# Keeping the MLP's residual in DRAM and adding it at the end, with 1/std spread over the partitions by a DMA instead of by TensorE

## The chip, the cores and the metric

One core of a Trainium2 chip runs one program: a decayed linear attention, an MLP behind a layer norm, and a small mixture of causal attention heads, all in float32 or in pairs of rounded float32 values. The metric is the device time of the program in microseconds.

## The reference, cut to what matters

```python
x = attn_out.transpose(0, 2, 1, 3).reshape(B, S, H * D)      # 2 x 768 x 512, output of the linear attention
mu  = np.mean(x, axis=-1, keepdims=True)
var = np.mean((x - mu) ** 2, axis=-1, keepdims=True)
xn  = (x - mu) / np.sqrt(var + 1e-06) * g_ln
x   = x + np.maximum(xn @ w_ch1, 0.0) @ w_ch2                # w_ch1: 512 x 2048, w_ch2: 2048 x 512
...                                                          # then gate, q, k, v, four attention heads, output product
```

Because ReLU commutes with a positive factor, `1/std` of a row can be put on the MLP's result instead of on its input: with `d = (x - mu) * g_ln`, the row's new `x` is `x + (relu(d @ w_ch1) @ w_ch2) / std`.

## The kernel before

Activations lie transposed in SBUF. The tile `xT` (`xpool`, line 309) holds all 1536 rows as 128 partitions x 4 slices of the model dimension x 1536 columns. The columns are four blocks of 384 (`TB`); `KS` (line 408) cuts the four slices into two halves, so that most VectorE and ScalarE work comes as 128 x 768 pieces (two slices of one block).

**Three stages.** First the linear attention (twelve steps `n`, one for each chunk of 128 rows), which ends with `ret_copy` (line 396): ScalarE copies from PSUM into `xT`. With it, as soon as a block of `xT` is whole, go the four norm steps `ln_a` to `ln_d` of that block, the preparation of weights (`prep_parts`, line 204) and the first MLP products. Second the MLP: `g1` (line 486) makes a group of the hidden layer, one `h` of 128 x 384 by 12 matmuls, and its `leave` turns it into the pair `hs` by ScalarE's ReLU and a VectorE subtraction; `g2` (line 519) multiplies four of these by the second weight, into a double PSUM bank `y` of 128 x 2 x 384, and its `leave` (line 532) adds `y` to `xT` on VectorE. The very first such sum, group 0 of block 0, is made piecemeal by `g2f` (line 539) in the two banks `yf0`, `yf1`. Third come the projections and the attention (`qkv_steps`, `att_s` and so on).

**The norm's factor.** `ln_d` (line 461) leaves `std` and `rs = 1/std` of a block as columns: 128 partitions x 3. `columns` (line 453) makes three matmuls with the identity out of such a column tile, which spread it as a row over all partitions in a PSUM tile (`sb` for std, `rb` for 1/std). Ahead of the block's first sum, `ln_e` (line 473) multiplies `xT` by std; the sums of all four groups are then added; `x2_split` (line 678) at the end multiplies by 1/std, and splits the result into the pair `x2` (ScalarE's cast, VectorE's subtraction, `split`, line 200). So residual and MLP sum live in one tile, at the price of one product ahead and one behind.

**What sets the order.** TensorE's order is that of the program text throughout. The other engines' order is the text's up to `by_hand.close()` (line 664) and a scheduler's after that. The weights come by SyncE's queue (`load_w`, line 122) into three buffers `raw` of pool `stage`; each is prepared in parts (`mag` on ScalarE, seven VectorE operations, the cast `w` on ScalarE), and the next load waits until VectorE has read the buffer. The PSUM tag `big` has two buffers, which `yf0`, `yf1` and then the `y` use in turn: a `y` can begin when the last but one has been taken out of PSUM.

Of the kernel before, what the change touches and what calls it, by code (L numbers as in the profile page):

```python
# [8 lines left out]
F32 = mybir.dt.float32  # L9
# [5 lines left out]
ALU = mybir.AluOpType  # L15
AX = mybir.AxisListType

P = 128
# [4 lines left out]
KT = DM // P  # L23
DFF = 2048
FT = DFF // P
TB = 384
NBLK = B * S // TB
NTB = TB // P
GF = 4
# [38 lines left out]
def model(ctx, tc, qkT, kv, lam, g_ln, w12, wat, out):  # L68
    nc = tc.nc
# [10 lines left out]
    stage = mp.enter_context(tc.tile_pool(name="stage", bufs=3))  # L80
    dec64 = mp.enter_context(tc.tile_pool(name="dec64", bufs=2))
    lnp = mp.enter_context(tc.tile_pool(name="lnp", bufs=2))
    psum = ctx.enter_context(tc.tile_pool(name="psum", bufs=1, space=bass.MemoryType.PSUM))
    dram = ctx.enter_context(tc.tile_pool(name="dram", bufs=1, space=bass.MemoryType.DRAM))
# [7 lines left out]
    def ps_mid(name):  # L92
        return psum.tile([P, 512], F32, tag="mid", bufs=4, name=name)
# [78 lines left out]
    n, free_at = PLAN_FROM, 0  # L172
    while rest:
        for p in rest:
            ft, i = p
# [5 lines left out]
        else:  # L181
            p = None
# [6 lines left out]
    pieces = first + [plan[n] for n in sorted(plan)]  # L189
    to_load = [lambda p=p: load_w(*p) for p in pieces] + [lambda i=i: load_wa(i) for i in range(4)]  # L190

    def load_next(k=1):
        for _ in range(k):
            if to_load:
                to_load.pop(0)()
# [4 lines left out]
    def split(dst_hi, dst_lo, src):  # L200
        nc.scalar.copy(dst_hi, src)
        nc.vector.tensor_tensor(dst_lo, src, dst_hi.bitcast(F32), ALU.subtract)
# [43 lines left out]
    second = []  # L246
# [157 lines left out]
            nc.scalar.copy(x[half(h2), 1], po[half(1 - h2), 1])  # L404


    XN, LN, DQ, SCALED = {}, {}, {}, set()
    KS = (ts(0, 2), ts(2, 4))

    def ln_parts(blk, src, name):  # L410
# [39 lines left out]
    def ln_c(blk):  # L450
        LN[blk] = ln_parts(blk, DQ[blk], "va")

    def columns(col, name):

        ps = ps_mid(name)
        for c in range(NTB):
            nc.tensor.matmul(ps[:, c * P:(c + 1) * P], col[:, c:c + 1].to_broadcast([P, P]), ident,
                             start=True, stop=True, skip_group_check=True)
        return ps[:, None, :TB].to_broadcast([P, 2, TB])

    def ln_d(blk):

        ps = ps_mid(f"var{blk}")
        for c in range(NTB):
            nc.tensor.matmul(ps[:, c:c + 1], LN[blk][:, c * P:(c + 1) * P], part_w[:, :1], start=True, stop=True,
                             skip_group_check=True)
        std = lnp.tile([P, NTB], F32, tag="std", name=f"std{blk}", bufs=NBLK)
        nc.scalar.activation(std, ps[:, :NTB], AF.Sqrt, bias=eps_sb)
        rs = lnp.tile([P, NTB], F32, tag="rs", name=f"rs{blk}", bufs=NBLK)
        nc.vector.reciprocal(rs, std)  # L470
        LN[blk] = (std, rs)

    def ln_e(blk):

        by = columns(LN[blk][0], f"sb{blk}")

        def times(ks):
            x = xT[:, ks, blk * TB:(blk + 1) * TB]
            nc.vector.tensor_tensor(x, x, by, ALU.mult)

        return [(1.0, lambda: times(KS[0])), (1.0, lambda: times(KS[1])), (0.0, lambda: SCALED.add(blk))]


    PASSES = ((0, 0), (1, 0), (0, 1))
    HS, LAST, HXT, HDQ = {}, [], [], []
# [33 lines left out]
    def g2(g, blk, half):  # L519

        y = ps_big(f"y{g}{blk}{half}")
        for f in range(GF):
            w = W[g * GF + f, 1]
            h = HS[g * GF + f, blk]
            for j in range(2):
                e = 2 * half + j
                for i, (wi, xi) in enumerate(PASSES):
                    nc.tensor.matmul(y[:, j, :TB], w[:, wi, e * P:(e + 1) * P], h[:, xi],  # L528
                                     start=(f == 0 and i == 0), stop=(f == GF - 1 and i == 2))
        xv = xT[:, 2 * half:2 * half + 2, blk * TB:(blk + 1) * TB]  # L530

        def leave():
            nc.vector.tensor_tensor(xv, xv, y[:, :, :TB], ALU.add)  # L533

        return leave

# [2 lines left out]
    def g2f(g, blk, f):  # L539

        if f == 0:
            YF.extend(ps_big(f"yf{j}") for j in range(2))
        w = W[g * GF + f, 1]
        h = HS[g * GF + f, blk]
        for e in range(KT):
            for i, (wi, xi) in enumerate(PASSES):
                nc.tensor.matmul(YF[e // 2][:, e % 2, :TB], w[:, wi, e * P:(e + 1) * P], h[:, xi],  # L547
                                 start=(f == 0 and i == 0), stop=(f == GF - 1 and i == 2))

        def leave():  # L550
            if f == GF - 1:
                for j in range(2):
                    xv = xT[:, 2 * j:2 * j + 2, blk * TB:(blk + 1) * TB]
                    nc.vector.tensor_tensor(xv, xv, YF[j][:, :, :TB], ALU.add)

        return leave

# [17 lines left out]
    def mlp_step():  # L575
        n = len(steps) - len(todo)
        due = [k for k in plan if k <= n]
        if due:
            plan.pop(min(due))
        decode(1 if due else 0)  # L580
        for blk in range(1, NBLK):
            if todo[0] == ("g2", 0, blk, 0):
                for _, scale in ln_e(blk):
                    scale()
        f, args, leave = step()
        leave()
        return f, args
# [4 lines left out]

    later_parts = []
    for ft in range(GF):
        if ft == GF - 1:
            later_parts.append((2.0, lambda: [f() for _, f in ln_e(0)]))
        later_parts += prep_parts(ft, 1)

    def room(us):
# [5 lines left out]
    def ready(k, inside):  # L605
        f, g, blk, j = todo[k]
        if f == "g1":
            return blk in XN and (g * GF + j, 0) in W and not (inside and (j, blk) in IN_WA)
        return f == "g2f" and (g * GF + j, 1) in W and (j < GF - 1 or blk in SCALED) and not inside

    def next_step(inside):

# [10 lines left out]
    while n < len(order) or min(norm_at) < 4 or norm_parts or weight_parts:  # L623
        if n < len(order):
            if n + 3 < len(order):
                ret_load(*order[n + 3])
                if n < 2:
                    load_next()
            if n + 1 < len(order):
                ret_scores(n + 1)  # L630
            ret_outer(n)
            ret_state(n)
            ret_inner(n)
            if n + 1 < len(order):
                ret_decay(n + 1)
            if n + 1 < len(order):
                ret_qd(n + 1)
            ret_sum(n)
            ret_copy(n)

        for blk in range(NBLK):
            if n >= NTB * (blk + 1) and norm_at[blk] < 4 and not (norm_at[blk] == 2 and blk not in XN) \
                    and not (norm_at[blk] == 1 and blk > 0 and norm_at[blk - 1] < 3):
                norm_parts += (ln_a, ln_b, ln_c, ln_d)[norm_at[blk]](blk) or []
                norm_at[blk] += 1
        if n < len(order):
            leave = next_step(True) if n >= MLP_FROM else None
            if n > 0:
                room(ROOM[leave is not None])
            if leave:  # L650
                leave()
        if n == len(order) - 1:
            rp.close()
            ap_ = ctx.enter_context(tc.tile_pool(name="ap", bufs=HX, side="right", reuse_waits="tile"))
            WPOOL2[0] = mp.enter_context(tc.tile_pool(name="wpool2", bufs=1, side="right", reuse_waits="tile"))
            weight_parts += later_parts
        if n >= len(order):
            for _ in range(2):
                leave = next_step(False)
                room(ROOM_MLP)  # L660
                if leave:
                    leave()
        n += 1
# [5 lines left out]
    def split_wa(i):  # L669
        raw, n = WRAW[i]  # L670
        w = ap_.tile([P, 2, 1040], F32R, tag="wa", name=f"wa{i}") if i < HX else             xnp.tile([P, 2, 1040], F32R, tag="dq", name=f"wa{i}", bufs=1)
        for c in (ts(0, 512), ts(512, n)):
            split(w[:, 0, c], w[:, 1, c], raw[:, c])
        WA.append(w[:, :, :n])
# [2 lines left out]

    def x2_split(blk):
        x2 = xnp.tile([P, 2, KT, TB], F32R, tag="xn", name=f"x2_{blk}")
        by = columns(LN.pop(blk)[1], f"rb{blk}")  # L680
        for ks in KS:
            x = xT[:, ks, blk * TB:(blk + 1) * TB]
            nc.vector.tensor_tensor(x, x, by, ALU.mult)
            split(x2[:, 0, ks], x2[:, 1, ks], xT[:, ks, blk * TB:(blk + 1) * TB])
        X2[blk] = x2

    wa_jobs = [lambda i=i: split_wa(i) for i in range(4)]
    while todo:
        f, args = mlp_step()
        if not pieces and not second and to_load:  # L690
            load_next()
        elif not pieces and not second and wa_jobs and len(todo) % 2 == 0:
            wa_jobs.pop(0)()
        if f == "g2" and args[0] == NG - 1 and args[2] == 1:
            x2_split(args[1])
    for job in wa_jobs:
        job()
# [274 lines left out]
```

## Time and profile before

| | us |
|---|---|
| median of 3 runs (474.23, 476.39, 476.47) | 476.39 |
| the profiled execution's own time | 477.41 |
| its span in the profile | 475.6 |
| TensorE busy (97% of the span) | 462.1 |
| VectorE busy (71%) | 340.0 |
| ScalarE busy (43%) | 202.9 |
| GpSimd busy (18%) | 86.0 |
| DMA: bytes read, written | 31.47 MB, 3.15 MB |

A row of the chain or of a timeline reads: start in us, duration in us, engine, line of the kernel, operation, output <- input, count, and in brackets the idle time of the engine ahead of it and what ended that. Several instructions may be merged into one row. Matmuls overlap in their records: one of the 128 x 128 identity products shows 274 ns, but they follow each other much closer, so the chain, not the busy time, tells what a matmul costs. SPq and ACTq are the queues' DMA instructions on SyncE and ScalarE. A float32 matmul appears as two records.

### The profile page before, as it was taken

How to read it: one execution, taken by the hardware profiler on the slowest of the kernel's cores; microseconds unless marked ns; L12 is line 12 of the kernel's file. 1: busy time of each engine (PE TensorE's matmuls, PEld its weight loads, DVE VectorE, ACT ScalarE, POOL GpSimd, SP SyncE). 2: the span in 40 equal slices, each digit the busy share in tenths (PEclk: the TensorE clock that was granted, in tenths of full speed). 3: DMA queues.
4: the chain of work that ended last, by engine and by line, in shares of the span. 5: the costliest groups of instructions: out<-in, count | busy, mean ns of one | idle time of the engine just before them, and what ended most of it. 6: DMA issues, size and time to landing. Idle time of an engine off the chain costs nothing.

```text
span 475.6 us, 9173 instructions
## 1 busy us (share of the span) xinstructions
PE 462.1 (97%) x3630; PEld 430.8 (91%) x3630; DVE 340.0 (71%) x707; ACT 202.9 (43%) x471; POOL 86.0 (18%) x132
## 2 busy tenths in 40 slices
PE   6799999999999999999999999999999999999996
PEld 4676779999999999999999999999998898998885
DVE  4688888979999787626789725435679686586663
ACT  2558675412334222202234312212356666647672
POOL 6556400000000000000000000000055444344340
PEclk8999999999999999999999999999999999999999
DMA  7986211222232231201233200000000000000011
GB/s 283 370 308 234 97 45 45 90 88 74 90 109 92 91 124 46 89 1 44 65 113 96 83 1 0 2 1 1 1 0 1 24 22 24 23 1 33 36 46 66
DMA packets 10842, 35.20 MB, mean 74 GB/s; under 512 B 1456, under 2 KB 1712, under 8 KB 10800
## 3 DMA queue, kind: packets, MB, share of 16 engines
q1 hardware_dynamic: 10512, 34.49, 21.1%
q8 instruction: 28, 0.46, 0.4%
q10 hardware_dynamic: 288, 0.13, 0.1%
q14 instruction: 14, 0.11, 0.1%
HBM read 31.47 MB, written 3.15 MB: 73 GB/s over the span
## 4 chain that ended last, share of the span: by engine, by line
PE 84%; DVE 9%; ACT 4%; DMA 1%; issue 1%; POOL 0%; SPq 0%; ACTq 0%; DVEq 0%
PE h L494 27%; PE y L528 26%; PE pj L730 4%; PE s L810 4%; PE av L859 4%; PE o L880 4%; PE t L847 4%; PE pv L752 3%; PE yf L547 2%; DVE a L347 2%; DMA qk<-in_qkT 1%; PE sc L326 1%; DVE xn L440 1%; PE po L378 1%; DVE qs L738 1%
## 5 line engine op out<-in xcount | busy, mean ns | idle before, releaser
L494 PE MATMUL h<-xn,w 128*128 128x384 f32 x768 | 140.0, 336 | 0.0
L494 PEld LDWEIGHTS h<-xn,w 128*128 128x128 f32 x768 | 133.3, 188 | 3.1 <-PE va L414 0.6
L528 PE MATMUL y<-hs,w 128*128 128x384 f32 x552 | 99.8, 334 | 0.0
L528 PEld LDWEIGHTS y<-hs,w 128*128 128x128 f32 x552 | 96.1, 188 | 0.0
L513 ACT ACTIVATE hs<-h 128x384 fp32r<-128x384 f32 x50 | 24.5, 490 | 103.0 <-PE h L494 89.4
L744 POOL TENSOR_SCALAR kh<-kh 64x384 fp32r<-64x384 f32 x16 | 8.4, 524 | 299.8 <-DVE qs L738 288.2
L514 DVE SCALAR_TENSOR_TENSOR hs<-h,hs 128x384 fp32r<-128x384 f32 x50 | 27.7, 555 | 41.4 <-ACT hs L513 41.4
L533 DVE TENSOR_TENSOR xT<-xT,y 128x768 f32<-128x768 f32 x30 | 28.5, 951 | 31.6 <-PE y L528 31.6
L837 POOL TENSOR_SCALAR att<-att,c,gw 128x128 f32<-128x128 f32 (+5 forms) x48 | 35.8, 750 | 51.7 <-DVE c L834 16.3
L229 ACT CAST w<-top 128x512 fp32r<-128x512 f32 x32 | 19.9, 620 | 52.9 <-DVE top L223 50.9
L730 PE MATMUL pj<-x,wa 128*128 128x384 f32 x192 | 35.0, 337 | 0.0
L730 PEld LDWEIGHTS pj<-x,wa 128*128 128x128 f32 x192 | 33.4, 188 | 0.0
L848 ACT COPY aT<-t 128x512 f32<-128x512 f32 (+3 forms) x64 | 26.5, 442 | 11.1 <-PE t L847 10.8
L847 PE MATMUL t<-ident,att 128*128 128x128 f32 x168 | 26.2, 275 | 0.5 <-DVE qs L738 0.5
L214 ACT ACTIVATE mag<-raw 128x512 f32<-128x512 f32 x32 | 21.1, 666 | 7.1 <-DVE w L241 7.1
L859 PE MATMUL av<-aT,v 128*64 128x128 f32 x336 | 23.6, 280 | 0.0
L810 PE MATMUL s<-kh,qs 128*128 128x512 f32 (+3 forms) x64 | 23.3, 366 | 0.0
L234 DVE SCALAR_TENSOR_TENSOR mag<-raw,mag 128x512 f32<-128x512 uint32 x32 | 22.8, 711 | 0.6
L238 DVE TENSOR_TENSOR top<-top,w 128x512 f32<-128x512 f32 x32 | 22.4, 700 | 0.0
L223 DVE SCALAR_TENSOR_TENSOR top<-raw,mag 128x512 int32<-128x512 int32 x32 | 22.0, 687 | 0.5
L241 DVE TENSOR_TENSOR w<-top,mag 128x512 fp32r<-128x512 f32 x32 | 22.0, 686 | 0.4
L859 PEld LDWEIGHTS av<-aT,v 128*64 128x64 f32 x336 | 17.8, 136 | 4.4 <-issue 3.9
(127 smaller groups left out, 720.4 us busy)
## 6 DMA issues: line engine op xcount, KB each, us to landing
raw<-in_w SPq DMA_DIRECT2D x32, 512.0 KB, 3.7
qk<-in_qkT SPq DMA_DIRECT2D x12, 512.0 KB, 6.2
kvn<-in_kv SPq DMA_DIRECT2D x12, 512.0 KB, 5.2
out<-os SPq DMA_DIRECT2D x11, 256.0 KB, 2.0
rawa<-in_wat SPq DMA_DIRECT2D x3, 512.0 KB, 3.2
rawa<-in_wat SPq DMA_DIRECT2D x1, 520.0 KB, 3.7
out<-os SPq DMA_DIRECT2D x1, 128.0 KB, 1.7
out<-os ACTq DMA_DIRECT2D x1, 128.0 KB, 1.7
```

What stands on the lines that cost most here:

```text
L234: nc.vector.scalar_tensor_tensor(mag, RAW[ft, i][:, :, 0].bitcast(U32), 2.0 ** -52, mag, ALU.mult, ALU.mult)
L494: nc.tensor.matmul(ph[:, :TB], w[:, wi, k, :], xn[:, xi, k, :], start=(i == 0), stop=(i == 11))
L513: LAST.append((nc.scalar.activation(h[:, 0], ph[:, :TB], AF.Relu), nc.vector.scalar_tensor_tensor(h[:, 1], ph[:, :TB], 0.0, h[:, 0].bitcas ...
L514: nc.vector.scalar_tensor_tensor(h[:, 1], ph[:, :TB], 0.0, h[:, 0].bitcast(F32), ALU.max, ALU.subtract)))
L528: nc.tensor.matmul(y[:, j, :TB], w[:, wi, e * P:(e + 1) * P], h[:, xi], start=(f == 0 and i == 0), stop=(f == GF - 1 and i == 2))
L533: nc.vector.tensor_tensor(xv, xv, y[:, :, :TB], ALU.add)
L730: nc.tensor.matmul(ps[:, :TB], w[:, wi, k, :], x2[:, xi, k, :], start=(i == 0), stop=(i == 11))
L810: nc.tensor.matmul(ps[:, c0:c1], q, kk[:, e, c0:c1], start=(i == 0), stop=(i == 1))
L837: nc.gpsimd.tensor_scalar(a[:, :n], a[:, :n], c, gw, ALU.mult, ALU.mult)
L847: nc.tensor.transpose(pt[:, (j - j0) * P:(j - j0 + 1) * P], a[:, j * P:(j + 1) * P], ident)
L848: nc.scalar.copy(aT[:, j0 * P:j1 * P], pt[:, :(j1 - j0) * P])
L859: nc.tensor.matmul(pav[e2 * HD:(e2 + 1) * HD, pr * P:(pr + 1) * P], v[:, j, e * HD:(e + 1) * HD], row["aT"][e][:, j * P:(j + 1) * P], star ...
```

## The change

`ln_e` and `columns` are gone, with the set `SCALED` that made the last `g2f` wait for the product by std. In their place:

- `park(blk)` stores a block of `xT` to a DRAM tile `xd`, from ScalarE's queue, three blocks at the last step but one of the linear attention and the fourth at the last.
- The first MLP sum of a block is copied over `xT` by ScalarE (`yf0`, `yf1`, and `y` of group 0) instead of being added by VectorE.
- `ln_d` writes 1/std of all blocks into one tile `rs`; `rows_of_rs` stores it to DRAM as rows (`rd`), element by element, and `load_rs` reads a row back with a partition stride of zero, which spreads it over 128 partitions (`by`).
- `load_x` reads half a block of the parked x into a `raw` buffer (`xr`), on SyncE's queue, behind the loads of the last weights.
- `x2_split` multiplies by `by` and then adds `xr`, one more 128 x 768 VectorE operation for each half.

```diff
     def ln_d(blk):
...
-        rs = lnp.tile([P, NTB], F32, tag="rs", name=f"rs{blk}", bufs=NBLK)
-        nc.vector.reciprocal(rs, std)
-        LN[blk] = (std, rs)
...
+        nc.vector.reciprocal(RS[:, blk], std)
+
+    XD = dram.tile([NBLK, P, KT, TB], F32, tag="xd", name="xd")
+
+    def park(blk):
+
+        nc.scalar.dma_start(XD[blk], xT[:, :, blk * TB:(blk + 1) * TB])
+
+    RS = lnp.tile([P, NBLK, NTB], F32, tag="rs", name="rs", bufs=1)
+    RD = dram.tile([NBLK, TB], F32, tag="rd", name="rd")
+
+    def rows_of_rs():
+
+        nc.sync.dma_start(RD.rearrange("b (c p) -> p b c", p=P), RS)
+
+    def load_rs(blk):
+        by = lnp.tile([P, TB], F32, tag="s4", name=f"by{blk}")
+        nc.sync.dma_start(by, RD[blk:blk + 1, :].to_broadcast([P, TB]))
+        XR[blk, "by"] = by[:, None, :].to_broadcast([P, 2, TB])
+
+    XR = {}
+
+    def load_x(blk, ks):
+        raw = stage.tile([P, 1040], F32, tag="raw", name=f"xr{blk}{ks.start}")
+        x = XR[blk, ks.start] = raw[:, :2 * TB].rearrange("p (k i) -> p k i", k=2)
+        nc.sync.dma_start(x, XD[blk, :, ks])
+        if ks.start == 0:
+            load_rs(blk)
...
         def leave():
-            nc.vector.tensor_tensor(xv, xv, y[:, :, :TB], ALU.add)
+            if g == 0:
+                nc.scalar.copy(xv, y[:, :, :TB])
+            else:
+                nc.vector.tensor_tensor(xv, xv, y[:, :, :TB], ALU.add)
...
                     xv = xT[:, 2 * j:2 * j + 2, blk * TB:(blk + 1) * TB]
-                    nc.vector.tensor_tensor(xv, xv, YF[j][:, :, :TB], ALU.add)
+                    nc.scalar.copy(xv, YF[j][:, :, :TB])
...
-        for blk in range(1, NBLK):
-            if todo[0] == ("g2", 0, blk, 0):
-                for _, scale in ln_e(blk):
-                    scale()
...
+        if n >= len(order) - 2 and n < len(order):
+            for blk in range(NBLK - 1) if n == len(order) - 2 else (NBLK - 1,):
+                park(blk)
...
     def x2_split(blk):
         x2 = xnp.tile([P, 2, KT, TB], F32R, tag="xn", name=f"x2_{blk}")
-        by = columns(LN.pop(blk)[1], f"rb{blk}")
+        by = XR[blk, "by"]
         for ks in KS:
             x = xT[:, ks, blk * TB:(blk + 1) * TB]
             nc.vector.tensor_tensor(x, x, by, ALU.mult)
+            nc.vector.tensor_tensor(x, x, XR[blk, ks.start], ALU.add)
             split(x2[:, 0, ks], x2[:, 1, ks], xT[:, ks, blk * TB:(blk + 1) * TB])
```

On TensorE the order is the same but for the eight calls of `columns`, which are gone. On three other queues the order moves.

SyncE's queue at the first loads of the second group's weights (`raw4_0` is w_ch1 of hidden slice 4), before and then with the change:

```order
L125 DMA raw4_0_1262<-in_w12 128x1024
L125 DMA raw5_0_1316<-in_w12 128x1024
L125 DMA raw6_0_1377<-in_w12 128x1024
L125 DMA raw7_0_1452<-in_w12 128x1024
L125 DMA raw4_1_1498<-in_w12 128x1024
```

```order
L125 DMA raw4_0_1266<-in_w12 128x1024
L474 DMA rd_158<-rs_157 128x12x1
L125 DMA raw5_0_1319<-in_w12 128x1024
L478 DMA by0_3028<-rd_158 128x384
L478 DMA by1_3059<-rd_158 128x384
L125 DMA raw6_0_1360<-in_w12 128x1024
L125 DMA raw7_0_1450<-in_w12 128x1024
L125 DMA raw4_1_1490<-in_w12 128x1024
```

The store `rd` and the two reads `by0`, `by1`, which need it, now stand ahead of the loads `raw6_0` and `raw7_0`.

ScalarE at the last steps of the linear attention (`dq2` is the norm's square of block 2, `po11` the last chunk's output), before and then with the change:

```order
L436 ACTIVATE xn2_995<-dq2_994,g_sb_114 128x384 x4
L442 ACTIVATE dq2_994<-dq2_994 128x768
L513 ACTIVATE hs1_0_1009<-h1_0_996 128x384
L402 COPY xT_155<-po11_1021 128x2x128
L404 COPY xT_155<-po11_1021 64x2x128 x2
L442 ACTIVATE dq2_994<-dq2_994 128x768
```

```order
L442 ACTIVATE dq2_995<-dq2_995 128x768
L519 ACTIVATE hs1_0_1010<-h1_0_997 128x384
L467 DMA xd_156<-xT_155 512x1x384 x3
L402 COPY xT_155<-po11_1025 128x2x128
L404 COPY xT_155<-po11_1025 64x2x128 x2
L442 ACTIVATE dq2_995<-dq2_995 128x768
L214 ACTIVATE mag3_0_1064<-raw3_0_391 128x512
L519 ACTIVATE hw1_1_1058<-h1_1_1045 128x384
L467 DMA xd_156<-xT_155 512x1x384
```

Three stores now stand ahead of the second square of block 2, a fourth a little behind it.

ScalarE at the MLP's first sums (`y011` is group 0, block 1, second half), before and then with the change:

```order
L229 CAST w4_0_1448<-top4_0_1443 128x512
L229 CAST w5_0_1494<-top5_0_1489 128x512
L214 ACTIVATE mag6_0_1528<-raw6_0_1377 128x512
L214 ACTIVATE mag7_0_1574<-raw7_0_1452 128x512
L229 CAST w6_0_1534<-top6_0_1529 128x512
```

```order
L229 CAST w4_0_1446<-top4_0_1441 128x512
L229 CAST w5_0_1486<-top5_0_1481 128x512
L540 COPY xT_155<-y010_1452 128x2x384
L214 ACTIVATE mag6_0_1520<-raw6_0_1360 128x512
L214 ACTIVATE mag7_0_1560<-raw7_0_1450 128x512
L540 COPY xT_155<-y011_1492 128x2x384
L229 CAST w6_0_1526<-top6_0_1521 128x512
L229 CAST w7_0_1566<-top7_0_1561 128x512
```

The copies that empty `y010` and `y011` now stand on ScalarE among the weight preparation; that of `y011` is behind two instructions that need `raw6_0` and `raw7_0`.

## Rows read from the trace of the kernel before

**Rows 1.** The page: busy time of each engine; DMA rate in 40 slices.
```profile
PE 462.1 (97%) x3630; PEld 430.8 (91%) x3630; DVE 340.0 (71%) x707; ACT 202.9 (43%) x471; POOL 86.0 (18%) x132
...
GB/s 283 370 308 234 97 45 45 90 88 74 90 109 92 91 124 46 89 1 44 65 113 96 83 1 0 2 1 1 1 0 1 24 22 24 23 1 33 36 46 66
```

**Rows 2.** Chain that ended last, 104 to 126 us: start, duration, what.
```profile
106.86 0.67 PE sb L457 x6
107.52 8.37 PE y L528 x48
115.89 0.67 PE sb L457 x6
116.56 8.35 PE y L528 x48
```

**Rows 3.** The same chain, 326 to 342 us.
```profile
335.87 0.67 PE rb L457 x6
336.54 4.33 PE pv L752 x36
```

**Rows 4.** Instructions on the tiles sb and rb.
```profile
L457 PE MATMUL sb<-ident,std x24: 270/275/275, 93.5 to 125.3; 128*128 128x128 f32 x24
...
L457 PE MATMUL rb<-ident,rs x24: 272/275/275, 287.8 to 336.3; 128*128 128x128 f32 x24
```

**Rows 5.** TensorE's waits: total, times, longest; the largest and the norm's.
```profile
PE sc L326 <- DVE a L347: 4.0, 4, 2.2
...
PE va L414 <- ACT dq L442: 0.5, 1, 0.5
```

**Rows 6.** ScalarE's timeline, 60 to 70 us.
```profile
62.99 2.14 ACT L436 ACTIVATE xn<-dq,g_sb 128x384 fp32r<-128x384 f32 x4 [1.73 <-DVE dq L434]
...
67.26 0.84 ACT L442 ACTIVATE dq<-dq 128x768 f32<-128x768 f32 x1
```

**Rows 7.** DMA instruction on ScalarE's queue: its duration in ns.
```profile
L271 ACTq DMA_DIRECT2D g_sb<-in_g_ln x1: 403/403/403, 0.7 to 0.7; - x1
```

**Rows 8.** Groups by shape on ScalarE and VectorE: busy us, mean ns.
```profile
L848 ACT COPY aT<-t 128x512 f32<-128x512 f32 x24 | 13.9, 585 | 5.8 <-PE t L847 5.5
L201 ACT CAST x<-xT 128x768 fp32r<-128x768 f32 x8 | 6.7, 832 | 23.0 <-DVE xT L683 23.0
...
L533 DVE TENSOR_TENSOR xT<-xT,y 128x768 f32<-128x768 f32 x30 | 28.5, 951 | 31.6 <-PE y L528 31.6
```

**Rows 9.** ScalarE's timeline, the preparation of w6_0 and w7_0.
```profile
115.44 0.67 ACT L214 ACTIVATE mag<-raw 128x512 f32<-128x512 f32 x1
118.90 0.68 ACT L214 ACTIVATE mag<-raw 128x512 f32<-128x512 f32 x1 [2.79 <-DVE w L241]
```

**Rows 10.** SyncE's queue: issue of raw6_0 and of raw7_0.
```profile
100.22 0.33 SPq L125 DMA_DIRECT2D raw<-in_w  x1
112.80 0.33 SPq L125 DMA_DIRECT2D raw<-in_w  x1
```

**Rows 11.** VectorE: 1/std of block 3; then, at the MLP's end, wa and block 0's first sum.
```profile
91.98 0.17 DVE L470 RECIPROCAL rs<-std 128x3 f32<-128x3 f32 x1
...
267.49 1.90 DVE L202 TENSOR_TENSOR wa<-rawa,wa 128x528 fp32r<-128x528 f32 x3
...
279.72 0.95 DVE L533 TENSOR_TENSOR xT<-xT,y 128x768 f32<-128x768 f32 x1 [3.02 <-PE y L528]
```

**Rows 12.** DMA issues: count, KB each, us from issue to landing.
```profile
raw<-in_w SPq DMA_DIRECT2D x32, 512.0 KB, 3.7
...
out<-os SPq DMA_DIRECT2D x1, 128.0 KB, 1.7
...
lq<-in_lam SPq DMA_DIRECT2D x1, 4.0 KB, 3.4
```

**Rows 13.** VectorE's timeline, the last x2_split.
```profile
336.78 1.81 DVE L683 TENSOR_TENSOR xT<-xT,rb 128x768 f32<-128x768 f32 x2
338.63 1.83 DVE L202 TENSOR_TENSOR x<-xT,x 128x768 fp32r<-128x768 f32 x2
```

More of the change, by code (lines that the diff above doesn't have):

```diff
@@ L404, in ret_copy @@
             nc.scalar.copy(x[half(h2), 1], po[half(1 - h2), 1])
-    XN, LN, DQ, SCALED = {}, {}, {}, set()
+    XN, LN, DQ = {}, {}, {}
     KS = (ts(0, 2), ts(2, 4))
@@ L451, in ln_c @@
         LN[blk] = ln_parts(blk, DQ[blk], "va")
[L453 to L459, printed above, removed]
     def ln_d(blk):
@@ L466, in ln_d @@
                              skip_group_check=True)
-        std = lnp.tile([P, NTB], F32, tag="std", name=f"std{blk}", bufs=NBLK)
+        std = lnp.tile([P, NTB], F32, tag="std", name=f"std{blk}")
         nc.scalar.activation(std, ps[:, :NTB], AF.Sqrt, bias=eps_sb)
-        rs = lnp.tile([P, NTB], F32, tag="rs", name=f"rs{blk}", bufs=NBLK)
-        nc.vector.reciprocal(rs, std)
-        LN[blk] = (std, rs)
[L473 to L481, printed above, removed]
+        nc.vector.reciprocal(RS[:, blk], std)
[17 more added lines that the diff above has]
+            load_rs(blk)
     PASSES = ((0, 0), (1, 0), (0, 1))
@@ L594, in model @@
     for ft in range(GF):
-        if ft == GF - 1:
-            later_parts.append((2.0, lambda: [f() for _, f in ln_e(0)]))
         later_parts += prep_parts(ft, 1)
@@ L608, in ready @@
             return blk in XN and (g * GF + j, 0) in W and not (inside and (j, blk) in IN_WA)
-        return f == "g2f" and (g * GF + j, 1) in W and (j < GF - 1 or blk in SCALED) and not inside
+        return f == "g2f" and (g * GF + j, 1) in W and not inside
     def next_step(inside):
@@ L683, in x2_split @@
             nc.vector.tensor_tensor(x, x, by, ALU.mult)
+            nc.vector.tensor_tensor(x, x, XR[blk, ks.start], ALU.add)
             split(x2[:, 0, ks], x2[:, 1, ks], xT[:, ks, blk * TB:(blk + 1) * TB])
         X2[blk] = x2
+    rows_of_rs()
     wa_jobs = [lambda i=i: split_wa(i) for i in range(4)]
+    x_loads = [lambda blk=blk, ks=ks: load_x(blk, ks) for blk in range(NBLK) for ks in KS]
     while todo:
@@ L691, in model @@
             load_next()
+        elif not pieces and not second and not wa_jobs and x_loads:
+            x_loads.pop(0)()
         elif not pieces and not second and wa_jobs and len(todo) % 2 == 0:
@@ L694, in model @@
         if f == "g2" and args[0] == NG - 1 and args[2] == 1:
+            while len(x_loads) > 2 * (NBLK - 1 - args[1]):
+                x_loads.pop(0)()
             x2_split(args[1])
```

## The prediction

> **What bounds the kernel now.** I read the page's busy times first, then the chain that ended last, then TensorE's waits. TensorE is busy for 462.1 of 475.6 us, VectorE for 340.0 and ScalarE for 202.9 [rows 1]. The chain shows what that means in the MLP: one `h`, `y` or column piece follows the other on TensorE with no hole between start plus duration of one and the start of the next (106.86 + 0.67 is 107.52 but for rounding, and 107.52 + 8.37 = 115.89) [rows 2]. The list of TensorE's waits holds only small sums, the largest 4.0 us for the decayed scores in the first stage [rows 5]. So from the first MLP products on, time is saved by taking matmuls away, and time is lost only where another engine makes TensorE wait that did not before.
>
> **What is taken from TensorE.** The eight `columns` calls stand in the chain as pieces of 0.67 us: `sb` at 106.86 and at 115.89 between two sums [rows 2], `rb` at 335.87 between the last sum and the first projection [rows 3]. There are 24 matmul records on each of `sb` and `rb`, so four calls of three two-record matmuls for each [rows 4]. The record's own 275 ns [rows 4] is not the price: six of them would be 1.65 us, yet the chain moves on after 0.67, because the records overlap. I take the chain's step: 8 x 0.67 = 5.4 us off the path. All eight lie on it, since nothing that follows them on TensorE waits for their result; it goes to VectorE.
>
> **What VectorE gains and loses.** Gone are eight products by std, and eight additions (two of `yf`, six of `y` in group 0); new are eight additions of `xr`. Each is 128 x 768 and costs 0.95 us [rows 8]: 16 x 0.95 less and 8 x 0.95 more, net 7.6 us less. The part that goes lies around 95 to 133 us, where VectorE prepares weights almost without a pause, but TensorE was not waiting for it there, so I count no gain. The part that comes lies behind 277 us, where VectorE waits 3 us for a sum [rows 11]: hidden. At the last block, VectorE had two products and two subtractions after the last sum's addition, 1.81 and 1.83 us [rows 13]; now the first half is done before the last sum ends, and behind it come one product, one addition, one cast of 0.83 us on ScalarE [rows 8] and one subtraction. That is the same to within 0.1 us, and its result is wanted much later: zero.
>
> **What ScalarE gains.** Eight copies of 768 columns out of PSUM. The trace has none of this size; 512 columns out of PSUM take 585 ns and 768 from SBUF 832 ns, VectorE's addition out of PSUM 951 ns [rows 8]. Bounds 0.6 and 0.95, I take 0.85, so 6.8 us in all on an engine that is idle more than half the time. They matter only through the two `big` buffers: the first half of block 2's sum reuses the buffer of `y010`, the second that of `y011`. With two columns less ahead, block 1's sums start at 107.52 - 1.34 = 106.2, take 8.37, and block 2's first half then takes 4.2, so its second half starts at 118.7 [rows 2]. `y011` is complete at 114.6, and its copy stands behind the two magnitudes `mag6_0` and `mag7_0`. In the old trace these ran at 115.44 and 118.90, the latter after a 2.79 us wait for VectorE [rows 9]. Ahead of what it waited for, VectorE had two products by std for block 1 and the additions of `y010` and `y011`, all four gone now; 4 x 0.95 us earlier, `mag7_0` comes at about 115.1 and the copy runs from 115.8 to 116.6. Against 118.7 that leaves 2.1 us: no wait, cost zero. This is the tightest place I find.
>
> **The four stores from ScalarE.** A DMA instruction on ScalarE's queue took 0.40 us [rows 7]. Three stand ahead of the second square of block 2, for which TensorE already waits 0.5 us [rows 5], and ScalarE works without a gap from 62.99 until that square ends at 68.1 [rows 6]. Upper bound: 3 x 0.40 = 1.2 us more wait, never made good. Lower bound: nothing, if the issuing runs ahead while the engine itself waits, as it did for 1.73 us just before 62.99 [rows 6]. No row shows which. I take 0.4, nearer to the lower end, because that pause is longer than the three issues. Their 3.1 MB move at 64 to 85 us, where the page shows 45 to 97 GB/s against 370 at its best [rows 1], and `xT` is not overwritten before the first sum, about 104 us: hidden.
>
> **The DMAs on SyncE's queue.** `rd` waits for 1/std of block 3, made at 92.1 [rows 11], and `raw5_0` was not issued before 94 anyway. Then `by0` waits until `rd` has landed, and `raw6_0` and `raw7_0`, once issued at 100.22 and 112.80 [rows 10], wait behind it. `rd` is 1536 single floats. The nearest row is `lq`, 1024 single floats read into SBUF in 3.4 us [rows 12]; by its bytes nothing at all is moved, so it lies between 1.7 us (the shortest landing of any load or store) and 1.5 x 3.4 = 5.1 us if count alone decides [rows 12]. I take 5.1, so `rd` lands at about 97.5 and `raw6_0` is not late. Cost zero. The parked x is read back into `raw` buffers after `wa` has been split, which ends at 269.4, and is wanted after the first sum of block 0, 279.7 before [rows 11] and some 277 now; a load four thirds its size lands in 3.7 us [rows 12], and there is no other traffic then (1 GB/s) [rows 1]: hidden.
>
> **The sum.** 477.41 - 5.4 + 0.4 = 472.4 us for the profiled execution. That execution was 1.0 us above the median of the three runs, 476.39, so against the median I forecast **471.4 us**, 1.0% faster.
>
> **The rivals.** First, *the copies make TensorE wait*. If a copy of 768 takes 0.95 us and VectorE gets ahead by 1 us there instead of 3.8, because it waits for ScalarE in its turn, `mag7_0` comes at 117.9, the copy ends at 119.5, and block 2's second half waits 0.8 us; the same hand-over holds block 3's two halves, so 1 to 3 us are lost in all: 472.4 to 474.4, and with the stores' upper bound 0.8 more. For it: VectorE and ScalarE hand each weight back and forth there. Against: VectorE loses far more work than ScalarE gains. Chance 0.14.
>
> Second, the other side, *the spread of 1/std holds SyncE's queue*. The single floats are written to DRAM, which no row shows. As long as `rd` is in flight, `by0` blocks the queue, `raw6_0` and `raw7_0` are late, `mag7_0` is late, and behind it stands the copy that frees `y011`'s buffer for TensorE. `raw7_0` has to land by 117.1 (118.7 less 0.95 less 0.67), so be issued by 113.4; `rd` may thus take from 92.2 to about 112, 20 us, before the first us is lost, and every further one is lost in full. At 25 us the gain is eaten; at 32 us the time is 471.4 + 12 = 483 us. Against: it needs five times what `lq` suggests. Chance 0.05. The Trainium skill, page "DMA: Bandwidth & Descriptors", section "Rules for kernel authors", speaks against such a store: a non-contiguous last dimension becomes one descriptor per element, and a rearranged access pattern used for a transposition is put at 19 times the hardware's one. Taken as an estimate from that page, 19 times the shortest landing of 1.7 us would be 32 us, the case just priced; the trace's `lq`, also a pattern of single floats at 3.4 us, does not agree with it on the reading side.
>
> Third, *nothing is gained*: the freed 5.4 us come back as waits elsewhere, because another engine paces the kernel a little behind TensorE, most likely in the attention stage, where VectorE and ScalarE hand the scores to TensorE. Then 475.5 to 476.5. Against it: the waits listed there are 0.5 us each and few [rows 5]. Chance 0.05. The forecast keeps 0.76.
>
> **How the numbers follow.** The forecast's own range is 470 to 472.6, from the stores' two bounds and the spread of runs (2.2 us among three). Adding the first rival's times, the range is 469.6 to 474.2; the other rivals and about a third of the first lie outside. About 0.5% (2.4 us) is what a measurement can tell from no change, so 474.0 divides faster from same: nearly all of the forecast and most of the first rival are faster, 0.85; the rest of both and the third rival are the same, 0.10; the second is slower, 0.05.
>
> **What the new profile should show.** No L457 row; `y` following `h` in the chain without a piece between; copies of `xT` out of `y` on ScalarE at 0.8 to 0.95 us; TensorE's wait for `dq` between 0.5 and 1.7 us; `rd` landing within about 6 us and `raw6_0` issued before 105; the `xr` loads landed before 277; VectorE's busy time about 332, ScalarE's about 210, TensorE's span shorter by 5. The prediction is wrong if TensorE's waits list a copy L540, if SyncE's queue shows a long stand at `by0`, or if the span falls by less than 3 us.

## The result, and the profile after

| | before | changed |
|---|---|---|
| median of 6 runs, us | 475.8 (474.23 to 477.19) | 471.94 (470.61 to 473.52) |
| ratio, 95% interval | | 0.9904 [0.9882, 0.9926] |
| span of the profiled execution, us | 475.6 | 470.5 |
| its own time, us | 477.41 | 472.28 |

The change makes the kernel 4.6 us faster by the ratio (3.5 to 5.6 us), 5.1 us by the two profiled spans. 471.4 had been forecast.

The page of the changed kernel, busy times, answers to [rows 1]:

```profile
PE 456.8 (97%) x3582; PEld 425.5 (90%) x3582; DVE 334.8 (71%) x699; ACT 208.9 (44%) x479; POOL 85.5 (18%) x132
```

TensorE has 48 records less and is busy 5.3 us less; ScalarE is busier by six, VectorE less by five. The chain that ended last, in the same two places as [rows 2, 3] (start, duration, what):

```profile
104.43 2.08 PE h L500 x12
106.51 20.87 PE y L534 x120
127.38 4.16 PE h L500 x24
...
331.36 4.32 PE pv L765 x36
```

Where `sb` had stood twice between pieces of `y`, 120 records of `y` now run without a break. TensorE's waits, the one that changed [rows 5]:

```profile
PE va L414 <- ACT dq L442: 1.0, 1, 1.0
```

It was 0.5. Why, ScalarE's timeline shows in the place of [rows 6]; ACTq rows are the four stores as ScalarE's instruction stream issues them:

```profile
63.71 0.59 ACTq L467 DMA_DIRECT2D xd<-xT  x1
...
64.33 0.65 ACTq L467 DMA_DIRECT2D xd<-xT  x1
...
65.02 1.41 ACTq L467 DMA_DIRECT2D xd<-xT  x1
...
66.47 0.37 ACT L402 COPY xT<-po 128x256 f32<-128x256 f32 x1 [0.40 <-issue]
...
67.63 0.84 ACT L442 ACTIVATE dq<-dq 128x768 f32<-128x768 f32 x1
```

The first two issues run beside products already queued on ScalarE. The third takes 1.41 us, ScalarE runs dry for 0.40 us, and the square that TensorE waits for comes that much later against its neighbours.

At the first sums, ScalarE's timeline (compare [rows 9]) and the DMA issues (count, KB each, us to landing, compare [rows 12]):

```profile
111.34 0.80 ACT L540 COPY xT<-y 128x768 f32<-128x768 f32 x1
112.96 0.68 ACT L214 ACTIVATE mag<-raw 128x512 f32<-128x512 f32 x1 [0.82 <-DVE w L241]
115.37 0.70 ACT L214 ACTIVATE mag<-raw 128x512 f32<-128x512 f32 x1 [1.73 <-DMA raw<-in_w]
115.96 0.80 ACT L540 COPY xT<-y 128x768 f32<-128x768 f32 x1
```

```profile
xd<-xT ACTq DMA_DIRECT2D x4, 768.0 KB, 6.0
xr<-xd SPq DMA_DIRECT2D x8, 384.0 KB, 3.3
...
by<-rd SPq DMA_DIRECT2D x4, 192.0 KB, 4.9
...
rd<-rs SPq DMA_DIRECT2D x1, 6.0 KB, 9.4
```

`y011`'s copy ends at 116.8; TensorE began to use its buffer again at 118.9. So the tightest place held. The 6 KB of `rd`, though, took 9.4 us to land, longer than a 768 KB store of `xd` (6.0 at the median), and `raw5_0`, issued behind it, landed 12.2 us after its issue (3.8 before):

```profile
DMA to landing us min/median/max: 12.2/12.2/12.2
```

(that row is line 125's issues of the changed kernel between 93 and 96 us). Nothing waited for it, by a margin that the experiments measure. SyncE's own waits show what the slow landing did to its queue (total, times, longest):

```profile
SPq L478 <- DMA rd<-rs: 7.3, 1, 7.3
```

So the queue did stand at `by0`, for 7.3 us.

**A ruler for the experiments.** The first 41 us are the same work in all these kernels, yet the `va` piece began anywhere from 39.5 to 42.3 us; the granted clock of 10 to 30 us was 0.88 in before and 1.00 in e6 and e2. So the kernels are compared by stretches of the chain: from the `va` piece near 41 us to the `h` piece of 24 records near 70 us (the end of the linear attention, with the stores), from there to the first `pv` piece (the MLP), and from `pv` to the span's end (the attention). One of the five runs of e6 took 507.22 us at a granted clock of 0.847 and is left out of its ratio; the other four took 472.05 to 474.85.

| | va to h | h to pv | pv to end |
|---|---|---|---|
| before | 27.81 | 266.90 | 139.06 |
| changed | 28.33 | 261.35 | 139.14 |
| e1, 1/std by TensorE | 28.33 | 264.11 | 139.80 |
| e6, 1/std by DMA alone | 27.82 | 264.11 | 138.88 |
| e3, columns twice | 27.83 | 272.13 | 139.11 |
| e2, stores from SyncE | 27.82 | 261.34 | 139.04 |
| e5, copies on VectorE | 28.48 | 261.34 | 139.12 |
| e7, stores twice | 34.05 | 261.44 | 139.05 |

Each is the difference of two starts in the chain; for before, 69.64 less 41.83, 336.54 less 69.64, and 475.6 less 336.54. The MLP lost 5.55 us, the end of the linear attention gained 0.52, the attention stayed.

### The profile page after: what moved, and what is told of

Same layout as the page of the kernel before. It is cut to its first block, busy times and chain, and to the rows that moved or that the text cites. A ratio compares the mean times of both kernels' runs of the same rounds, so it can differ in the third digit from the quotient of the medians.

```text
span 470.5 us, 9124 instructions
## 1 busy us (share of the span) xinstructions
PE 456.8 (97%) x3582; PEld 425.5 (90%) x3582; DVE 334.8 (71%) x699; ACT 208.9 (44%) x479; POOL 85.5 (18%) x132
## 2 busy tenths in 40 slices
DMA packets 16234, 42.28 MB, mean 90 GB/s; under 512 B 3264, under 2 KB 6080, under 8 KB 16192
## 4 chain that ended last, share of the span: by engine, by line
PE 83%; DVE 9%; ACT 4%; DMA 1%; issue 1%; ACTq 0%; SPq 0%; POOL 0%; DVEq 0%
PE h L500 27%; PE y L534 27%; PE s L823 4%; PE av L872 4%; PE o L893 4%; PE t L860 4%; PE pj L743 3%; PE pv L765 3%; PE yf L556 2%; PE sc L326 1%; DVE a L347 1%; DMA qk<-in_qkT 1%; DVE qs L751 1%; PE po L378 1%; DVE xn L440 1%
## 5 line engine op out<-in xcount | busy, mean ns | idle before, releaser
L542 DVE TENSOR_TENSOR xT<-xT,y 128x768 f32<-128x768 f32 x24 | 22.8, 951 | 27.6 <-PE y L534 27.6
```

## The experiments

**Theory T:** from the first MLP products TensorE sets the pace, each column call costs its place in the chain, and the stores cost what they delay ScalarE. **Rival V:** the gain comes from VectorE's lighter load in the first sums, and the column calls were as good as free.

### e1: 1/std spread by TensorE again

```diff
-        by = XR[blk, "by"]
+        by = columns(RS[:, blk], f"rb{blk}")
...
-    rows_of_rs()
```

`load_rs` is gone as well; parking and ScalarE's copies stay.

> The changed kernel with 1/std spread by TensorE again (four column calls, PSUM row instead of the DMA's row); parking, reloading and ScalarE's copies stay. Theory T (TensorE paces, each column call costs its 0.67 us of the chain): span 470.5 + 4 x 0.67 = 473.2 us, each rb piece again 0.67 us in the chain, ratio to the kernel before about 0.995. Rival V (the gain comes from VectorE's lighter load in the first sums, the column calls were as good as free): span stays at 470.5, ratio 0.990.

Measured: 473.06 us, ratio 0.9924 [0.9901, 0.9947], span 473.4. The chain has the piece back:

```profile
326.00 6.94 PE y L540 x40
332.94 0.67 PE rb L457 x6
333.60 4.33 PE pv L770 x36
```

The MLP stretch is 2.76 us longer than in the changed kernel, 0.69 for each of four calls. VectorE has the same work in the first sums as in the changed kernel, so V would have the stretch unchanged: V falls for this half. (The attention is 0.7 us longer here, with a wait of 0.6 for a GpSimd copy that no other run shows.)

### e6: 1/std by the DMA alone

The kernel before, with `rows_of_rs` and `load_rs`; products by std, `sb`, and additions stay.

```diff
-        by = columns(LN.pop(blk)[1], f"rb{blk}")
+        by = XR[blk, "by"]
```

> The kernel before with only 1/std spread by the DMA; products by std, additions on VectorE and the sb column calls stay, nothing is parked. T: span 475.6 - 4 x 0.67 = 472.9 us, TensorE's wait for dq stays at 0.5 us, ratio 0.994. V: VectorE's load is that of before, so 475.6, ratio 1.000. If the DMA's spreading held SyncE's queue at a cost, the span would be above 472.9 and TensorE would show a wait for h or y operands behind raw6_0 and raw7_0.

Measured: 474.72 us, ratio 0.9932 [0.9906, 0.9958]. The span of its profiled execution, 470.3, is 2.6 below what was expected, but its `va` piece began at 39.5 us against 41.8 before; the MLP stretch is the 264.11 of e1, 2.79 less than before, and TensorE's wait for `dq` is 0.5. Again 0.70 a call, now with VectorE's first sums as they were. The two halves of the change add up: 2.79 us from before to e6, where only `rb` goes, and 2.76 from e6 to the changed kernel, where `sb` goes and VectorE's first sums become lighter, 5.55 together. So e1 and e6 both single out `rb`; whether the other half comes from `sb` or from VectorE's load, e3 and e5 have to tell.

### e3: every column call twice

```diff
+        columns(LN[blk][0], f"sc{blk}")
         by = columns(LN[blk][0], f"sb{blk}")
...
+        columns(LN[blk][1], f"rc{blk}")
         by = columns(LN.pop(blk)[1], f"rb{blk}")
```

> The kernel before with every column call made twice (eight more, whose results nobody reads). T: span 475.6 + 8 x 0.67 = 481.0 us, ratio 1.011. V: within 1 us of 475.6, because the pieces would fit into time that TensorE has to spare.

Measured: 482.44 us, ratio 1.0099 [1.0069, 1.0129], span 480.3. The chain, here around the first pair:

```profile
91.01 2.08 PE h L495 x12
93.09 0.67 PE sc L457 x6
93.76 0.67 PE sb L457 x6
94.43 2.09 PE yf L548 x12
```

The MLP stretch grew by 5.23 us, 0.65 a call. Four of the eight extra calls stand at the places of `sb`: from the `h` piece near 70 us to the first one behind the last `sb` the chain took 60.14 us before (69.64 to 129.78) and takes 62.75 here (69.06 to 131.81), 2.61 more. T is confirmed from the other side, and for both halves: pieces of 0.67 us that nobody needs lengthen the kernel nearly in full.

### e2: the stores from SyncE's queue

```diff
-        nc.scalar.dma_start(XD[blk], xT[:, :, blk * TB:(blk + 1) * TB])
+        nc.sync.dma_start(XD[blk], xT[:, :, blk * TB:(blk + 1) * TB])
```

> The changed kernel with the four stores of x issued from SyncE's queue instead of ScalarE's. T: TensorE's one longer wait (va for dq, 1.0 us against 0.5 before) came from the issues standing in ScalarE's instruction stream; it falls back to 0.5 us, span 470.0 us, ratio 0.989. Rival (the wait comes from the stores' traffic or from run to run): it stays at 1.0 us and the span at 470.5. Rival (SyncE's queue pays instead): raw2_1 is issued later than 72.3 us and a wait for its weights appears; not expected, since SyncE idles from 60.5 to 72.3 us.

Measured: 471.72 us beside 477.36 of before, ratio 0.9882 [0.9861, 0.9904], span 468.8. TensorE's wait is back:

```profile
PE va L414 <- ACT dq L442: 0.5, 1, 0.5
```

The stretch from `va` to `h` is the 27.82 of the kernels without stores, 0.51 us less than with them on ScalarE. The bytes are the same, though issued from 59.3 us on instead of 63.7; with ScalarE's 0.40 us of idle time at the third issue, and with e7 below, this puts the cost on the issuing. `raw2_1` was issued at 71.1 and landed in 3.5 us: SyncE paid nothing. By the chain this version is 0.5 us faster than the changed kernel; by the medians the two cannot be told apart, since their intervals overlap.

### e7: every block stored twice from ScalarE

```diff
+        nc.scalar.dma_start(XE[blk], xT[:, :, blk * TB:(blk + 1) * TB])
         nc.scalar.dma_start(XD[blk], xT[:, :, blk * TB:(blk + 1) * TB])
```

> The changed kernel with each block of x stored twice from ScalarE's queue, to two places. With no store from ScalarE the stretch from the va pieces near 41 us to the h pieces near 70 us was 27.8 us, with four 28.3. T (the issues stand in ScalarE's stream; the first of them hide beside work queued already, which runs out about at the end of the third): three more issues of 0.6 to 1.4 us ahead of the square are exposed in full, the wait for dq 2.8 to 4.5 us, the stretch 30.1 to 31.8. Rival (the 0.5 us is a fixed cost of a first store, or of the traffic): 28.3 to 28.8.

Measured: one time, 478.59 us, span 476.8. ScalarE's timeline in the place shown above:

```profile
65.62 1.41 ACTq L468 DMA_DIRECT2D xe<-xT  x1
...
67.07 1.44 ACTq L469 DMA_DIRECT2D xd<-xT  x1
68.54 1.44 ACTq L468 DMA_DIRECT2D xe<-xT  x1
70.01 1.43 ACTq L469 DMA_DIRECT2D xd<-xT  x1
71.49 0.37 ACT L402 COPY xT<-po 128x256 f32<-128x256 f32 x1 [4.82 <-issue]
```

The wait for `dq` is 5.4 us and the stretch 34.05, more than the upper end expected, because all three further issues took 1.4 us, none 0.6. The direction is T's: they are exposed in full (3 x 1.44 = 4.3 us), and the fixed-cost rival falls. The stretch grew by another 1.4 us, for which a further store at the fourth block and a slower clock (0.70 granted between 71 and 76 us, after TensorE had waited) may stand; that is argued, not shown.

### e5: the first outputs copied by VectorE

```diff
-                nc.scalar.copy(xv, y[:, :, :TB])
+                nc.vector.tensor_copy(xv, y[:, :, :TB])
```

and the same for `yf`.

> The changed kernel with the first outputs (two yf, six y) copied by VectorE instead of ScalarE. T (neither engine sets the pace there): the stretch from h at 70.0 to the first pv stays at 261.35 us within 0.2, ratio 0.990; VectorE about 6 us busier, ScalarE 6.4 us less. Rival V (it pays to take these off VectorE): the stretch grows by 1 us or more, with a wait of TensorE at y020 to y031 for a copy.

Measured: 472.25 us, ratio 0.9902 [0.9885, 0.992]. The MLP stretch is 261.34 us. A copy of 768 columns takes VectorE 950 ns and ScalarE 800 ns (the L540 groups by shape, first of e5, then of the changed kernel):

```profile
L540 DVE COPY xT<-y 128x768 f32<-128x768 f32 x6 | 5.7, 950 | 0.0
```

```profile
L540 ACT COPY xT<-y 128x768 f32<-128x768 f32 x6 | 4.8, 800 | 2.2 <-PE y L534 2.2
```

Which engine makes them is worth nothing here: VectorE takes 5.7 us of work back in the first sums and the stretch stays, so V falls for the other half too. The eight products by std were not put back by themselves; against them speaks that the chain before has no hole in the first sums [rows 2] that less work on VectorE could have closed. In neither version does TensorE wait for a copy, so the prediction's first rival falls too.

### e4 and e8: the store of 1/std three and five times

```diff
+        for i in range(2):
+            more = dram.tile([NBLK, TB], F32, tag=f"rm{i}", name=f"rm{i}")
+            nc.sync.dma_start(more.rearrange("b (c p) -> p b c", p=P), RS)
         nc.sync.dma_start(RD.rearrange("b (c p) -> p b c", p=P), RS)
```

(e8 with `range(4)`.) The extra stores are read by nobody.

> The changed kernel with the store of 1/std made three times, the reads by0 and by1 waiting for the third. It prices the rival of the held queue. The one store was issued at 92.5 us and landed 9.4 us later, and nothing waited for it. The stretch of the chain from the h pieces at 70.0 us to the first pv piece was 261.35 us. Theory T (lost from the point at which y011's copy ends after TensorE wants the buffer, 119.1 us; raw7_0 lands about 5 us after the last store does, magnitude and copy take 1.5 us more): a third landing at about 112.5 us costs nothing, every us behind it is lost; with some 8 us for each store it lands at 116 to 118, so TensorE waits 4 to 5.5 us at y021 for ScalarE's copy, the stretch is 265 to 267, the ratio to the kernel before about 0.999. Rival (weights have 10 us and more of slack, a late load costs nothing): 261.35 and 0.990.

> The same with five stores. T: each further store's time is lost in full, so 2 x 8 = 16 us more than with three: TensorE's wait at y021 some 20 us, the stretch 281 to 283, slower than the kernel before. Rival (slack): no more than a few us.

e4 measured: 485.29 us, ratio 1.0172 [1.0157, 1.0187]; e8, one time, 497.23 us. So a slow spread of 1/std does turn the change into a loss, as the prediction's second rival had it, but sooner and at another place. Both expectations were too low: the MLP stretch is 275.0 us in e4 (265 to 267 expected) and 287.1 in e8 (281 to 283), and the two further stores of e8 cost 12.1 us, not 16. In e8 `raw5_0` was issued ahead of the fifth store. In e4 the third store landed 25.3 us after its issue, at 118.4. The chain that ended last shows what was late:

```profile
93.94 26.66 DMA raw<-in_w
...
120.69 0.67 ACT mag L214
...
124.24 0.80 ACT xT L543
...
125.08 15.29 PE y L537 x72
```

That is `raw5_0`, issued right behind the stores, not `raw6_0` or `raw7_0`. `mag5_0` waits for it, behind `mag5_0` on ScalarE stands the copy of `y010`, and TensorE needs `y010`'s buffer for the first half of block 2 (its timeline):

```profile
125.08 4.21 PE L537 MATMUL y<-hw,w 128*128 128x384 f32 x12 [10.91 <-ACT xT L543]
```

The loss is larger than the wait. These twelve records took 4.21 us; in the changed kernel they took 2.26. Stretches of e4 (first their length, then busy times, TensorE's first; the last three columns are granted clock, DMA share and GB/s) show the clock at half in the pause and still there when TensorE starts again at 125.1. The last two rows are of TensorE alone:

```profile
112.00:118.00 6.00, 2.17 (x13) 1.86 (x11) 0.00 (x0) 0.00 (x0) 0.00 (x0) 0.91 0.66 36
118.50:122.00 3.50, 0.00 (x0) 0.00 (x0) 0.62 (x2) 0.66 (x1) 0.00 (x0) 0.50 0.63 162
...
125.00:130.00 5.00, 4.92 (x15) 0.50 0.59 209
130.00:134.00 4.00, 4.00 (x23) 0.93 0.39 134
```

From the `h` ahead of `y010` to `pv`, TensorE's timelines give 240.8 us in e4 and 227.1 in the changed kernel: 13.7 more, 10.9 of waiting and 2.8 beside it. Of these, 2.6 lie in the next 24 records, which took 6.78 us from their first start to the next piece's (125.08 to 131.86) against 4.18 (114.69 to 118.87). In e8 TensorE waited 21.9 us in two pieces, of 18.8 and 3.1.

The margin follows: in the changed kernel `raw5_0` landed at 106.5, in e4 at 120.6, 14.1 later, and 10.9 us were lost. So only some 3 us were to spare (the copy of `y010` ended at 112.1 in the changed kernel, and TensorE began to use that buffer again at 114.7), not the 20 us for the store that the prediction had worked out for `raw7_0`.

### e9: the three stores from ScalarE's queue

```diff
-        nc.sync.dma_start(RD.rearrange("b (c p) -> p b c", p=P), RS)
+        nc.scalar.dma_start(RD.rearrange("b (c p) -> p b c", p=P), RS)
```

and so for the two extra ones.

> The kernel with three stores of 1/std, now all issued from ScalarE's queue; the reads by0 and by1 stay on SyncE's. With the stores on SyncE's queue TensorE waited 10.9 us at y020, because raw5_0, issued behind them on the same queue, landed only 2 us after the last of them, and mag5_0 stands ahead of y010's copy. Theory Q (the load suffers from its place behind the stores on one queue): raw5_0 now lands within about 6 us, mag5_0 follows mag4_0 near 107 us and no wait at y020 remains; by0 still waits until the third store has landed (some 118 us), so raw6_0 and raw7_0 land at 123 to 124, y011's copy ends near 125, and TensorE waits about 7 us at y021, which it wants at 118.2. Rival D (single floats clog the 16 DMA engines whatever the queue): raw5_0 lands near 120 again, 10 to 11 us of wait at y020.

Measured: one time, 488.9 us. ScalarE's wait for `raw5_0`:

```profile
123.53 0.66 ACT L214 ACTIVATE mag<-raw 128x512 f32<-128x512 f32 x1 [15.92 <-DMA raw<-in_w]
```

The load, on the other queue now, still took 29.2 us to land, and TensorE waited 13.1 us at the first half of block 2 and 1.7 at the second. Theory Q falls: the delay does not come from the place in one queue, a load on another queue has it as well. That is what rival D expected, though its word for the cause, clogged DMA engines, is not shown; by what means the stores hold back the load, these runs don't tell.

## Why the prediction was right, step by step

- **TensorE's part** held: 5.4 us forecast for the eight calls, 5.55 measured (0.69 each, since the piece behind a call is also some hundredths longer: 8.37 and 4.19 us for pieces that otherwise take 8.32 and 4.16). e1 and e6 show it as cause for `rb`, and e3 for both halves by doubling; that the half of `sb` does not come from VectorE's lighter load rests on e3, e5 and the chain without holes.
- **VectorE and ScalarE at nothing** held. The MLP stretch does not change when the copies move between them (e5). `y011`'s copy was forecast from 115.8 to 116.6 and ran from 115.96 to 116.76, its buffer wanted at 118.9 against a forecast of 118.7. One reason was wrong: `mag7_0` had waited for its load in the end, 1.73 us, not for VectorE.
- **The stores' issuing** was taken at 0.4 between bounds of 0 and 1.2; e2 puts it at 0.51. Right by balance: two issues were hidden as argued, but one took 1.41 us where [rows 7] had 0.40.
- **The spread of 1/std** is the step that failed, though it cost nothing. The store was put between 1.7 and 5.1 us by the count of `lq`; it took 9.4. That count was misread: `lq` is not 1024 single floats. The page before counts its packets:

```profile
DMA packets 10842, 35.20 MB, mean 74 GB/s; under 512 B 1456, under 2 KB 1712, under 8 KB 10800
...
q1 hardware_dynamic: 10512, 34.49, 21.1%
```

q1 is SyncE's queue, with 73 transfers: 144 packets for each, its 128 rows and 16 small ones more (the store of 1536 floats shows 1552). `lq` is one of them, so it came in 128 packets of 8 floats. The small packets say the same: 16 for each of the 75 transfers of both queues are 1200 of the 1456 under 512 B, and the other 256 are the rows of `lq` and `g_sb`, 128 each. So the store's 1536 pieces were 12 times `lq`'s, not 1.5 times, and no row of before priced a transfer of single floats in either direction. The prediction looked for the harm behind `by0`, at `raw6_0` and `raw7_0`, with 20 us to spare. e4 shows it at the load that is in flight beside the store, `raw5_0`, with about 3 us to spare. At a landing time of 25 us the prediction had the gain just eaten; at 25.3 us e4 was 1.7% slower than before. The rival's direction and its last link (a `y` buffer emptied late) were right; it priced 5.3 us for such a landing, and e4 lost 13.7. Its chance of 0.05 rested on the size taken from `lq`, so that the one store stayed harmless, by some 3 us, was luck. The stand at `by0`, which the prediction had named as a sign of being wrong, did show (7.3 us) and cost nothing.

- **The rule of the Trainium skill** (page "DMA: Bandwidth & Descriptors", section "Rules for kernel authors") that such a store falls apart into one descriptor per element agrees with the page of the profile: packets under 512 B were 3264 in the changed kernel and 6368 in e4, 1552 for each further store of 1536 floats. Its factor of 19 for a transposing pattern, worked out in the prediction to 32 us as an estimate, was too high for this store, which landed in 9.4 us. `lq`, which the prediction held against it, says nothing on it, since it is no pattern of single floats.
- **Nothing gained in the attention** was the third rival; `pv` to the end is 139.06 us before and 139.14 after, so what TensorE gained in the MLP was kept to the end.

## What to carry to other kernels

Where one engine's chain has no holes, price a step by its place in that chain (0.67 us for records of 1.65 in sum), and look for cover only on the others. A few kilobytes of single floats can hold back half-megabyte loads that are in flight beside them, on the same queue (e4) and on another (e9): price such a store by what is in flight, not only by who waits for it. Before a row is taken as the price of such a store, count its packets. Issue a store of many short rows from an engine that has nothing due behind it.

## What the runs showed of the hardware

- 1536 single floats from SBUF to DRAM landed in 9.4 us in the changed kernel, and in 9.5 to 11.3 in e2, e5, e6 and e7, which store them once too. Each further store of the kind on SyncE's queue pushed the last landing back by about 8.2 us (from 101.9 to 118.4 us for two more), while the DMA engines moved few bytes: this row is a stretch of the changed kernel within the store (last columns clock, DMA share, GB/s).

```profile
94.50:98.00 3.50, 3.50 (x22) 3.50 (x21) 3.36 (x8) 0.71 (x2) 0.00 (x0) 1.00 0.04 5
```

- A load issued right behind them lands late: 512 KB took 12.2 us with one store, 26.7 with three on its own queue and 29.2 with three on the other queue, against 3.8.
- A DMA instruction's own time is not fixed. A store of 512 rows took 0.59 and 0.65 us for the first two, and 1.41 to 1.47 for those that followed at once (e7 has five of them; the changed kernel's fourth, 1.2 us after the third, took 0.52); loads of 128 rows take 0.33. A load behind three stores of single floats took 3.33 us to issue.
- In e4, in a pause of 10.9 us, TensorE's granted clock fell to 0.50 of 2.4 GHz, the 1.2 GHz level, and it was 0.50 over the 5 us after work began again; beside the pause itself 2.8 us were lost. A stall of that length cost more than itself.
